# Chunk-selected attention into a gated causal convolution: from merged step lists to a list-scheduled graph, with the convolution in sixteen 32x32 array tiles

## The chip, the core and the metric

The kernel runs on one core of a Trainium2 chip. TensorE (PE) multiplies matrices, with weight loads of its own (PEld); VectorE (DVE), ScalarE (ACT) and GpSimd (POOL) work elementwise; SyncE (SP) issues the DMAs. PE writes to PSUM, eight banks of 512 fp32 numbers on each of 128 partitions, from which DVE and ACT read. The metric is the time of one execution on the device in microseconds.

## The reference

Inputs are q, k, v of shape (4, 8, 768, 64) and the weights w_val, w_out (512x512) and conv_w (5x512). Keys are cut into 24 chunks of 32. Each query takes the six chunks with the highest upper bound among its causal ones, and attends to their keys:

```python
k_min, k_max = k_chunks.min(3), k_chunks.max(3)
ub = sum(maximum(q * k_min, q * k_max), axis=-1)       # per query and chunk
ub = where(causal, ub, -1e9);  top_chunks = argsort(ub)[..., -6:]
scores = q @ k.T / 8;  mask = (chunk of key in top_chunks) & causal
x = softmax(where(mask, scores, -1e9)) @ v             # heads side by side: (4, 768, 512)
gate = sigmoid(sum_k conv_w[k] * x shifted by 4 - k)   # per channel, causal
out = (gate * (x @ w_val)) @ w_out
```

## The kernel before

The 32 heads are worked off as 16 pairs, two heads of one batch side by side on 128 partitions (64 each). Four pairs make a batch, whose 512 channels are four blocks of 128.

For each pair, `kq_steps` transposes k and q on PE in fp32 (lines 155 and 178). ACT copies keys, scaled, into KE (159) and q into q32 (181), GpSimd casts q to fp16 into QU (183) and v into VA (190), and DVE reduces each chunk of keys to maximum and minimum straight from PSUM (163, 164) and makes of them the fp32 operand KB (170, 172). `sel_steps` computes all bounds with fp32 matmuls (207 with relu(q), 209 with q), takes the eight highest with `max` (219), compares with the sixth (224), transposes the 0/1 result (233) and copies it into the free rows of QU (236). There it meets the rows of KE that hold -30 for each chunk, so that the score matmul (271) adds the penalty of chunks that are not selected. `attn_steps` takes exp of a 512-column bank at a time (275, 295), GpSimd zeroes the triangle above the diagonal (264, 280), `av` multiplies with v and a column of ones (304), DVE divides (306, 307), and six transposes put the pair into xT (314, 316).

For each batch, `moe_gate` does the convolution on PE: five taps, each a diagonal 128x128 matrix in two fp16 parts (high and rest), so ten accumulating matmuls of 384 columns for each block and half of the sequence (334); ACT takes tanh (339). `moe_val` multiplies with w_val (348) and DVE forms the gate product (352). `moe_out` multiplies with w_out (359), ACT evacuates (362), SP stores (363). The 40 diagonals are built once by GpSimd in `moe_diag` (379), ten in each of the first four pairs; the cast of the weights is also GpSimd's (366, 367).

The order of the work is written by hand: `merge` interleaves the step lists of the attention of pair i, the selection of pair i+1, the transposes of pair i+2 and the batch steps due then, by their relative place in each list. PSUM has three pools: three banks for scores, two for AV, three for all the rest. Six loads for each pair are issued by SP, two pairs ahead.

Of the kernel before, what the change touches and what calls it, by code (L numbers as in the profile page):

```python
# [13 lines left out]
AX = mybir.AxisListType  # L14


@with_exitstack
def kernel(
# [10 lines left out]
    nc = tc.nc  # L29
# [8 lines left out]
    PEN = -30.0  # L38
    NPAIR = (B * H) // 2
    HB = S // 2  # L40


    HP = (slice(0, 64), slice(64, 128))
    CP = (slice(64, 64 + NCH), slice(0, NCH))
    KP = (slice(0, 64 + NCH), slice(0, 128))

    CC = (1, 0)
    SELT = NT - 1

    ident_np = np.eye(128, dtype=np.float32)  # L50
    identh_np = np.eye(128, dtype=np.float16)
    e_np = np.zeros((64, S), dtype=np.float16)
    for c in range(NCH):
        e_np[c, c * CH:(c + 1) * CH] = PEN
    cfill_np = np.zeros((128, SELT, 2, NCH), dtype=np.float32)
    for it in range(1, NT):
        for p in range(128):
            cfill_np[p, it - 1, :, (it * 128 + p) // CH + 1:] = -1.0e9
    cfill_np = cfill_np.reshape(128, SELT * 2 * NCH)

    ident_dr = nc.inline_tensor(ident_np, name="identc")
    identh_dr = nc.inline_tensor(identh_np, name="identh")
    e_dr = nc.inline_tensor(e_np, name="echunk")
    cfill_dr = nc.inline_tensor(cfill_np, name="cfill")

    cpool = ctx.enter_context(tc.tile_pool(name="cpool", bufs=1))
    npool = ctx.enter_context(tc.tile_pool(name="npool", bufs=3))
    hpool = ctx.enter_context(tc.tile_pool(name="hpool", bufs=2))
    ppool = ctx.enter_context(tc.tile_pool(name="ppool", bufs=2))
    mpool = ctx.enter_context(tc.tile_pool(name="mpool", bufs=2))  # L70
    ps = ctx.enter_context(tc.tile_pool(name="ps", bufs=3, space=bass.MemoryType.PSUM))

    ident = cpool.tile([128, 128], FP, tag="ident")
    identh = cpool.tile([128, 128], F16, tag="identh")
    cfill = cpool.tile([128, SELT * 2 * NCH], FP, tag="cfill")
    wval_sb = cpool.tile([128, NCT, DM], F16, tag="wval")
    wout_sb = cpool.tile([128, NCT, DM], F16, tag="wout")
    w32 = cpool.tile([128, 2, NCT, DM], FP, tag="w32")
    cwn = cpool.tile([KSZ * NCT, 128], FP, tag="cwn")
    cwT = cpool.tile([128, KSZ * NCT], FP, tag="cwT")  # L80
    cwh = cpool.tile([128, KSZ * NCT], F16, tag="cwh")
    cwl = cpool.tile([128, KSZ * NCT], FP, tag="cwl")
    diag = cpool.tile([128, KSZ * NCT, 2, 128], F16, tag="diag")
    xT = cpool.tile([128, 2 * NCT, S + 4], F16, tag="xT")
    KE = [cpool.tile([128, 2, S], F16, tag=f"KE{i}", name=f"KE{i}") for i in range(3)]
    QU = [cpool.tile([128, 2, S], F16, tag=f"QU{i}", name=f"QU{i}") for i in range(3)]
    VA = [cpool.tile([128, 2, NT, D + 1], F16, tag=f"VA{i}", name=f"VA{i}") for i in range(3)]
    KB = [cpool.tile([128, 2, 2 * NCH], FP, tag=f"KB{i}", name=f"KB{i}") for i in range(2)]
    NS = [cpool.tile([128, SELT, 128], F16, tag=f"NS{i}", name=f"NS{i}") for i in range(2)]

    def bank(shape, dt=FP, tag="w", bufs=3):
        return ps.tile(shape, dt, tag=tag, name=f"ps_{tag}", bufs=bufs)

    nat = {}

    def load_kq(p):
        b, h0 = p // NCT, 2 * (p % NCT)
        kn = npool.tile([128, NT, 128], FP, tag="kn", name="kn")
        qn = npool.tile([128, NT, 128], FP, tag="qn", name="qn")
        vn = npool.tile([128, NT, 128], FP, tag="vn", name="vn")  # L100
        nat[p] = (kn, qn, vn)
        for t, src in ((kn, k), (qn, q)):
            for hh in range(2):
                nc.sync.dma_start(out=t[:, :, hh * 64:(hh + 1) * 64],
                                  in_=src[b, h0 + hh].rearrange("(t p) d -> p t d", p=128))

    def load_v(p):
        b, h0 = p // NCT, 2 * (p % NCT)
        for hh in range(2):
            nc.sync.dma_start(out=nat[p][2][:, :, hh * 64:(hh + 1) * 64],  # L110
                              in_=v[b, h0 + hh].rearrange("(t p) d -> p t d", p=128))


    nc.sync.dma_start(out=ident, in_=ident_dr.ap())
    load_kq(0)
    for i in range(3):
        for hh in range(2):
            nc.sync.dma_start(out=KE[i][HP[1 - hh], hh, :], in_=e_dr.ap())
    nc.sync.dma_start(out=cfill, in_=cfill_dr.ap())
    nc.sync.dma_start(out=identh, in_=identh_dr.ap())  # L120
    load_v(0)
    load_kq(1)
    load_v(1)
    nc.sync.dma_start(out=cwn, in_=moe_conv_w.rearrange("k (c p) -> (k c) p", p=128))
    nc.sync.dma_start(out=w32[:, 0], in_=moe_w_val.rearrange("(ct c) e -> c ct e", c=128))
    nc.sync.dma_start(out=w32[:, 1], in_=moe_w_out.rearrange("(et e) o -> e et o", e=128))

    for i in range(2):
        nc.gpsimd.memset(KB[i], 0.0)
    for i in range(3):  # L130
        nc.vector.memset(QU[i][HP[1], 0, :], 0.0)
        nc.vector.memset(QU[i][HP[0], 1, :], 0.0)
    for i in range(2):
        nc.gpsimd.memset(NS[i], 0.0)
    for i in range(3):
        nc.gpsimd.memset(VA[i][:, :, :, D:D + 1], 1.0)
    nc.vector.memset(xT[:, :, 0:4], 0.0)

    st = {}


    def kq_steps(p):
        kn, qn, vn = nat.pop(p)
        ke, qu, va, kb = KE[p % 3], QU[p % 3], VA[p % 3], KB[p % 2]
        kmx = hpool.tile([128, NCH], FP, tag="kmx", name="kmx")
        kmn = hpool.tile([128, NCH], FP, tag="kmn", name="kmn")
        kmd = hpool.tile([128, NCH], FP, tag="kmd", name="kmd")
        q32 = hpool.tile([128, S], FP, tag="q32", name="q32")
        rq = hpool.tile([128, S], FP, tag="rq", name="rq")
        st[p] = dict(ke=ke, qu=qu, va=va, kb=kb, q32=q32, rq=rq)  # L150

        def khalf(w):
            pt = bank([128, HB])
            for tl in range(3):
                nc.tensor.transpose(out=pt[:, tl * 128:(tl + 1) * 128],  # L155
                                    in_=kn[:, 3 * w + tl, :], identity=ident)
            sl = slice(w * HB, (w + 1) * HB)
            for hh in range(2):
                nc.scalar.activation(out=ke[HP[hh], hh, sl], in_=pt[HP[hh]],  # L159
                                     func=AF.Copy, scale=0.125)  # L160
            cs = slice(w * 12, (w + 1) * 12)
            ptc = pt.rearrange("p (c t) -> p c t", t=CH)
            nc.vector.tensor_reduce(out=kmx[:, cs], in_=ptc, axis=AX.X, op=ALU.max)  # L163
            nc.vector.tensor_reduce(out=kmn[:, cs], in_=ptc, axis=AX.X, op=ALU.min)

        def kblock():
            nc.vector.tensor_tensor(out=kmd, in0=kmx, in1=kmn, op=ALU.subtract)
            for hh in range(2):
                hp, c0 = HP[hh], CC[hh] * NCH
                nc.vector.tensor_scalar(out=kb[hp, 0, c0:c0 + NCH], in0=kmd[hp],  # L170
                                        scalar1=kmd[hp, 0:1], scalar2=None, op0=ALU.subtract)
                nc.vector.tensor_scalar(out=kb[hp, 1, c0:c0 + NCH], in0=kmn[hp],
                                        scalar1=kmn[hp, 0:1], scalar2=None, op0=ALU.subtract)

        def qhalf(w):
            pt = bank([128, HB])
            for tl in range(3):
                nc.tensor.transpose(out=pt[:, tl * 128:(tl + 1) * 128],  # L178
                                    in_=qn[:, 3 * w + tl, :], identity=ident)
            sl = slice(w * HB, (w + 1) * HB)  # L180
            nc.scalar.activation(out=q32[:, sl], in_=pt, func=AF.Copy)  # L181
            for hh in range(2):
                nc.gpsimd.tensor_copy(out=qu[HP[hh], hh, sl], in_=q32[HP[hh], sl])  # L183
            a = max(w * HB, 128)
            nc.vector.tensor_scalar(out=rq[:, a:(w + 1) * HB], in0=q32[:, a:(w + 1) * HB],
                                    scalar1=0.0, scalar2=None, op0=ALU.max)

        def vcast():
            for hh in range(2):
                nc.gpsimd.tensor_copy(out=va[:, hh, :, 0:D],  # L190
                                      in_=vn[:, :, hh * 64:(hh + 1) * 64])

        return [lambda: khalf(0), lambda: khalf(1), lambda: qhalf(0), kblock, lambda: qhalf(1),
                vcast]
# [254 lines left out]
```

## Time and profile before

| | |
|---|---|
| median of 3 runs | 294.87 us (294.83 to 296.1) |
| profiled execution, first to last instruction | 292.5 us |
| median less that span | 2.4 us |
| mean granted TensorE clock | 0.959 |
| PE busy / PEld busy | 241.3 / 171.6 us |
| DVE / ACT / POOL busy | 155.2 / 160.2 / 121.8 us |
| read and written in HBM | 21.79 and 6.29 MB |

The profiled execution has its span as its own time; the runs' times include what lies around it. Lines such as L334 are lines of the kernel before. A group's row gives the operation, its output and input, its count, then its busy time in us, the mean ns of one, and the idle time in front with what ended it. Matmuls are pipelined: the mean of one is its latency, and the price of one in a row of many is read from a timeline, as length over count.

### The profile page before, as it was taken

The numbers are of one execution on the slowest core, as the hardware profiler recorded it, in microseconds if no ns is written. First come the engines' busy times: TensorE is split into PE (matmuls) and PEld (weight loads), VectorE is DVE, ScalarE is ACT, GpSimd is POOL, SyncE is SP. The second block draws the span as 40 slices with busy tenths as digits, with TensorE's granted clock in tenths as the row PEclk, the third lists the DMA queues.
The fourth block names the chain that finished last, engine by engine and source line by source line (L and its number), as shares of the span: only waits on it lengthen the run. The fifth ranks groups of instructions, "written<-read, shape, count | busy, mean of one in ns | idle before, by whom it ended". The sixth has DMA issues, their size and how long they took to land.

```text
span 292.5 us, 5928 instructions
## 1 busy us (share of the span) xinstructions
PE 241.3 (82%) x2161; PEld 171.6 (59%) x2161; DVE 155.2 (53%) x522; ACT 160.2 (55%) x329; POOL 121.8 (42%) x261
## 2 busy tenths in 40 slices
PE   2383926509998897999998999999989999999994
PEld 1181614405757575776666667676757676765551
DVE  3547162404676674858573657666645667631160
ACT  3232713503768659465674774756747765467313
POOL 2416189999254436243433253425251624223000
PEclk9999975956999999999999999999999999999999
DMA  7999992205162554242456343332211000003105
GB/s 165 211 304 245 218 175 54 54 0 110 33 132 55 110 110 99 66 108 56 107 151 159 91 114 86 70 87 61 74 74 38 36 2 0 2 2 143 73 2 215
DMA packets 80746, 28.46 MB, mean 97 GB/s; under 512 B 75962, under 2 KB 76622, under 8 KB 80718
## 3 DMA queue, kind: packets, MB, share of 16 engines
q1 hardware_dynamic: 80718, 28.09, 40.9%
q8 instruction: 17, 0.28, 0.4%
q14 instruction: 11, 0.09, 0.1%
HBM read 21.79 MB, written 6.29 MB: 96 GB/s over the span
## 4 chain that ended last, share of the span: by engine, by line
PE 66%; POOL 12%; ACT 10%; issue 3%; SPq 3%; DVE 2%; DMA 2%; ACTq 0%; POOLq 0%
PE ps_w L334 17%; PE ps_s L271 10%; POOL diag L379 7%; PE ps_av L304 6%; PE ps_w L348 6%; PE ps_w L359 6%; PE ps_w L209 6%; ACT P L275 5%; PE ps_w L207 5%; PE ps_w L155 4%; PE ps_w L178 2%; POOL QU L183 2%; PE ps_w L314 2%; ACT KE L159 2%; ACT osb L362 1%
## 5 line engine op out<-in xcount | busy, mean ns | idle before, releaser
L275 ACT ACTIVATE P<-ps_s 128x512 f16<-128x512 f32 x160 | 87.8, 606 | 57.1 <-PE ps_s L271 56.8
L271 PE MATMUL ps_s<-QU,KE 88*128 88x512 f16 (+5 forms) x224 | 54.9, 336 | 7.1 <-ACT P L275 4.1
L264 POOL TENSOR_SCALAR_AFFINE_SELECT P<-P 128x256 f16<-128x256 f16 (+1 forms) x80 | 29.0, 364 | 71.1 <-ACT P L275 58.3
L334 PE MATMUL ps_w<-xT,diag 128*128 128x384 f16 x320 | 57.8, 331 | 0.0
L304 PE MATMUL ps_av<-VA,P 128*128 128x65 f16 x672 | 33.4, 196 | 21.9 <-POOL P L264 19.9
L304 PEld LDWEIGHTS <-P 128*128 128x128 f16 x672 | 28.4, 99 | 32.0 <-POOL P L264 26.2
L159 ACT ACTIVATE KE<-ps_w 64x384 f16<-64x384 f32 x64 | 31.0, 485 | 26.9 <-PE ps_w L155 26.5
L183 POOL CAST QU<-q 64x384 f16<-64x384 f32 x64 | 35.1, 548 | 24.6 <-ACT q L181 22.7
L334 PEld LDWEIGHTS <-diag 128*128 128x128 f16 x320 | 31.0, 99 | 21.4 <-issue 1.9
L339 ACT ACTIVATE g<-ps_w 128x384 f32<-128x384 f32 x32 | 15.9, 498 | 30.5 <-PE ps_w L334 30.5
L209 PE MATMUL ps_w<-KB,q 128*128 128x48 f32 x160 | 32.3, 285 | 0.0
L163 DVE TENSOR_REDUCE kmx<-ps_w 128x12 f32<-128x384 f32 x32 | 17.8, 555 | 26.7 <-ACT KE L159 26.6
L236 DVE COPY QU<-ps_w 24x640 f16<-24x640 f16 x32 | 15.5, 484 | 29.9 <-PE ps_w L233 29.4
L207 PE MATMUL ps_w<-KB,rq 128*128 128x48 f32 x160 | 31.2, 278 | 0.0
L271 PEld LDWEIGHTS <-KE 88*128 88x128 f16 (+1 forms) x224 | 21.1, 101 | 16.8 <-issue 10.8
L280 POOL TENSOR_SCALAR_AFFINE_SELECT P<-P 128x256 f16<-128x256 f16 x32 | 13.1, 408 | 31.4 <-ACT P L275 31.3
L207 PEld LDWEIGHTS ps_w<-KB,rq 128*128 128x128 f32 x160 | 25.9, 202 | 0.3
L155 PE MATMUL ps_w<-ident,kn 128*128 128x128 f32 x96 | 17.7, 300 | 9.7 <-DMA kn<-in_k_dram 9.7
L209 PEld LDWEIGHTS ps_w<-KB,q 128*128 128x128 f32 x160 | 25.7, 202 | 0.0
L348 PE MATMUL ps_w<-xT,wval_sb 128*128 128x384 f16 x128 | 23.9, 325 | 1.8 <-ACT q L181 1.8
L190 POOL CAST VA<-vn 128x384 f16<-128x384 f32 x32 | 16.5, 516 | 20.4 <-PE ps_av L304 12.9
L359 PE MATMUL ps_w<-wout_sb,gv 128*128 128x512 f16 x96 | 23.8, 379 | 0.7 <-ACT osb L362 0.7
(46 smaller groups left out, 309.0 us busy)
## 6 DMA issues: line engine op xcount, KB each, us to landing
kn<-in_k_dram SPq DMA_DIRECT2D x32, 192.0 KB, 3.3
qn<-in_q_dram SPq DMA_DIRECT2D x32, 192.0 KB, 3.4
vn<-in_v_dram SPq DMA_DIRECT2D x32, 192.0 KB, 3.3
out_dram<-osb SPq DMA_DIRECT2D x24, 256.0 KB, 2.0
w<-in_moe_w_val_dram SPq DMA_DIRECT2D x1, 1024.0 KB, 5.6
w<-in_moe_w_out_dram SPq DMA_DIRECT2D x1, 1024.0 KB, 7.9
KE<-echunk SPq DMA_DIRECT2D x6, 96.0 KB, 2.7
cfill<-cfill SPq DMA_DIRECT2D x1, 120.0 KB, 2.3
```

The source lines that it names most:

```text
L155: nc.tensor.transpose(out=pt[:, tl * 128:(tl + 1) * 128], in_=kn[:, 3 * w + tl, :], identity=ident)
L159: nc.scalar.activation(out=ke[HP[hh], hh, sl], in_=pt[HP[hh]], func=AF.Copy, scale=0.125)
L183: nc.gpsimd.tensor_copy(out=qu[HP[hh], hh, sl], in_=q32[HP[hh], sl])
L207: nc.tensor.matmul(out=pu[:, it - 1, :], lhsT=rq[:, ts], rhs=kb[:, 0, :], start=True, stop=False)
L209: nc.tensor.matmul(out=pu[:, it - 1, :], lhsT=q32[:, ts], rhs=kb[:, 1, :], start=False, stop=True)
L264: nc.gpsimd.affine_select(out=ap, in_=ap, pattern=[[0, n], [1, 128]], compare_op=ALU.is_ge, fill=0.0, base=0, channel_multiplier=-1)
L271: nc.tensor.matmul(out=pq[:, col:col + n], lhsT=ke[KP[hh], hh, jt * 128:(jt + 1) * 128], rhs=qu[KP[hh], hh, q0:q0 + n], start=True, stop=True)
L275: nc.scalar.activation(out=pt, in_=pq, func=AF.Exp)
L304: nc.tensor.matmul(out=pav[:, qt, :], lhsT=where[hh, jt, qt], rhs=va[:, hh, jt, :], start=(jt == 0), stop=(jt == qt))
L334: nc.tensor.matmul(out=pg, lhsT=diag[:, ki * NCT + ct, part, :], rhs=xT[:, slot, w * HB + ki:w * HB + ki + HB], start=(n == 0), stop=(n == ...
L348: nc.tensor.matmul(out=pv, lhsT=wval_sb[:, ct, et * 128:(et + 1) * 128], rhs=xT[:, slot0 + ct, 4 + w * HB:4 + (w + 1) * HB], start=(ct == ...
L359: nc.tensor.matmul(out=po, lhsT=gv[b, et][:, s * 128:(s + 1) * 128], rhs=wout_sb[:, et, :], start=(et == 0), stop=(et == NCT - 1))
```

## The change

The kernel is written anew. Every operation is added to a `Plan` as a node with an engine, a duration and a latency (constants in the file), a priority (pair number times `PERIOD` plus an offset for its kind from `OFF`), the tiles that it reads and writes, and the PSUM banks that it takes. `Plan.schedule` places the nodes one after another: of those ready on an engine, the earliest, by priority among equals; banks are given out of all eight as nodes need them. The instructions are then emitted in the order of their planned starts.

```diff
+    def schedule(self):
...
+                if best is None or t < best[0]:
+                    best = (t, n, pick)
...
+        return sorted(done, key=lambda n: (n.start, n.i))
...
+    order = plan.schedule()
+    with tc.manual_schedule():
+        for n in order:
+            n.fn()
-    merge(kq_steps(0))
-    merge(sel_steps(0), kq_steps(1))
```

The convolution waits for all four pairs of a batch, takes four banks, and runs as 160 matmuls for each half of the sequence, each on a 32x32 tile of the array. Row tile r takes channels 32r to 32r+31 of each block; column tile c is block c; each row tile writes its own bank. So gate channels come out in another order, and the columns of w_val and the rows of w_out are permuted to match when they are cast and loaded. The diagonals shrink to 32x32 and are built by DVE in two instructions.

```diff
-                    nc.tensor.matmul(out=pg, lhsT=diag[:, ki * NCT + ct, part, :],
-                                     rhs=xT[:, slot, w * HB + ki:w * HB + ki + HB],
-                                     start=(n == 0), stop=(n == 2 * KSZ - 1))
+                for n in range(2 * KSZ):
+                    ki, part = n // 2, n % 2
+                    for r in range(4):
+                        rp = slice(32 * r, 32 * r + 32)
+                        for c in range(4):
+                            nc.tensor.matmul(out=psum[32 * c:32 * c + 32, gb[r // 2].at + r % 2, 0:HB],
+                                             lhsT=diag[rp, part, ki * NCT + c, :],
+                                             rhs=xT[rp, s0 + c, hw * HB + ki:hw * HB + ki + HB],
+                                             start=(n == 0), stop=(n == 2 * KSZ - 1))
```

The bounds are computed in fp16: q is split into a high part QH and a rest QL, relu(q) into RH and RL, the key bounds likewise, and six matmuls of 48 columns for each of five query tiles (two for the first) replace two fp32 ones.

```diff
-                nc.tensor.matmul(out=pu[:, it - 1, :], lhsT=rq[:, ts], rhs=kb[:, 0, :],
-                                 start=True, stop=False)
-                nc.tensor.matmul(out=pu[:, it - 1, :], lhsT=q32[:, ts], rhs=kb[:, 1, :],
-                                 start=False, stop=True)
+                for lhs, part, kind in ((QH, 0, 1), (RH, 0, 0), (QH, 1, 1), (RH, 1, 0), (QL, 0, 1), (RL, 0, 0)):
+                    term(it, lhs, kbs(part, kind), n == 0, n == 5)
```

Who does what also moves. ACT evacuates keys and q in one 768-column instruction each; DVE reduces keys from that SBUF copy; GpSimd scales it into KE; DVE makes QH, RH, RL and QU, GpSimd QL:

```diff
+            add(f"ke{h}_{p}", POOL, t_pool(S), 100, base + OFF["KE"] + h,
+                lambda h=h: nc.gpsimd.tensor_scalar(out=KE[t3][HP[h], h, :], in0=K32[w][HP[h]],
+                                                    scalar1=0.125, scalar2=None, op0=ALU.mult),
...
+            lambda: nc.vector.tensor_copy(out=QH[w], in_=Q32[w]), [("Q32", w)], [("QH", w)])
...
+            lambda: nc.gpsimd.tensor_tensor(out=QL[w][:, 128:S], in0=Q32[w][:, 128:S],
+                                            in1=QH[w][:, 128:S], op=ALU.subtract),
```

Maxima and comparison read the bounds in PSUM, and the future chunks are filled there by one small addition. The two heads' score banks lie side by side, so exp takes 1024 columns at once (six instructions for a pair, eleven before), one GpSimd instruction zeroes the triangles of both heads, and one DVE instruction each divides, and forms the gate product for both halves. A 33rd selection row carries a shift of the scores by the row's highest bound; the first query tile, which had no selection, has it now too. One of the two mask copies is ACT's. Identities, chunk rows and fill are made on GpSimd, not loaded. Eight matmuls on zeros stand in front. Input tiles have four buffers, loads are issued up to 3.85 periods ahead, the weights' loads at 4.94 periods.

## The prediction

> **What bounds the kernel now.** I read the busy times first, then the table of windows, which says in which stage an engine is full, then the timeline of one steady stretch for the price of each operation. The page:
>
> ```profile
> PE 241.3 (82%) x2161; PEld 171.6 (59%) x2161; DVE 155.2 (53%) x522; ACT 160.2 (55%) x329; POOL 121.8 (42%) x261
> ```
>
> The 82% is a mean over unlike stages. The windows (length, then busy time of each engine) separate them:
>
> ```profile
> core 0: us, PE busy (x) PEld busy (x) DVE busy (x) ACT busy (x) POOL busy (x), PEclk, DMA share, GB/s
> 0.00:27.10 27.10, 10.99 (x50) 9.25 (x51) 14.51 (x43) 7.02 (x13) 10.04 (x24) 1.00 1.03 232
> 27.10:65.50 38.40, 19.18 (x150) 13.83 (x150) 11.56 (x46) 14.42 (x30) 29.56 (x54) 0.76 0.61 107
> 123.80:183.70 59.90, 56.73 (x542) 41.15 (x540) 37.95 (x129) 39.26 (x84) 23.28 (x53) 1.00 0.43 107
> 183.70:243.70 60.00, 56.82 (x543) 41.14 (x541) 37.25 (x130) 39.36 (x84) 23.00 (x52) 1.00 0.19 54
> 274.80:292.50 17.70, 13.67 (x77) 7.23 (x74) 4.44 (x8) 5.16 (x9) 0.00 (x0) 1.00 0.32 120
> ```
>
> Three stages: a start, in which PE is half idle up to 65.5 us (chain first, then GpSimd, 29.56 of 38.40 us); a steady part of 60 us for each batch of four pairs, in which PE is 95% busy and the others at two thirds or less; a tail. In the steady part removed PE work is removed time. Its prices, from the chain and the timeline (start, length, what):
>
> ```profile
> 123.81 3.26 PE ps_w L334 x20
> 127.34 0.66 PE ps_av L304 x21
> 132.26 1.31 PE ps_w L348 x8
> 204.92 0.86 PE ps_w L359 x4
> ```
>
> ```profile
> 129.60 0.50 PE L155 MATMUL ps_w<-ident,kn 128*128 128x128 f32 x3
> 129.93 0.32 PE L207 MATMUL ps_w<-KB,rq 128*128 128x48 f32 x2
> 132.10 1.47 PE L348 MATMUL ps_w<-xT,wval_sb 128*128 128x384 f16 x8
> ```
>
> So a 384-column matmul takes 163 ns, a 512-column one 216, an AV matmul (65 columns, with its own weight load) 31.5, an fp32 transpose 110 (129.60 to 129.93), and the bound matmuls of a pair 2.17 us (129.93 to 132.10). Last, two rows for the engines that share memory with each other:
>
> ```profile
> L379 POOL TENSOR_SCALAR diag<-identh,cwT 128x128 f16<-128x128 f16 x20 | 12.9, 647 | 0.0
> L185 DVE TENSOR_SCALAR rq<-q x32: 273/375/2045, 9.1 to 244.9; 128x256 f32<-128x256 f32 x16, 128x384 f32<-128x384 f32 x16
> ```
>
> The forty diagonal builds are what starves PE in the second window. The 2045 ns of a copy whose median is 375 falls beside GpSimd's 2067 ns cast of the weights: VectorE's plain SBUF copies stand still while GpSimd holds that memory.
>
> **Part by part.** *PE for a pair, before:* 12 fp32 transposes 1.32, bounds 2.17, five selection transposes 0.28, scores 2.28 (twice 2,688 columns at 0.42 ns), AV 42 x 31.5 = 1.32, six transposes 0.34: 7.7 us. A batch adds the convolution 80 x 163 = 13.0, value 32 x 163 = 5.2 and output 24 x 216 = 5.2, so 4 x 7.7 + 23.4 = 54.2 us of the 59.9: PE works 0.91 of the steady stretch by these prices.
>
> *Bounds in fp16 halves:* 32 fp16 matmuls of 48 columns with 128-column weights replace ten fp32 ones. Nearest row is AV: 32 x 31.5 = 1.0 us, 1.2 less. With six selection transposes, a pair costs 6.6 us; 16 pairs 105.8.
>
> *The convolution:* 40 full matmuls for each half of a sequence and channel block become 160 matmuls for all four blocks, each 32x32 with its own 32-column weight load; 1280 in all. No row shows such a tile. If all 16 stream together, ten rounds of 163 ns make 10.2 ns each; if they are limited by issuing load and matmul, the nearest row is AV's 31.5, an upper bound in so far as its load is four times wider; if they run one after another, 163. I take 26, by AV's row less something for the narrower load: 1280 x 26 = 33.3 us against 52.2 now. Ends 13 and 40 if they overlap; 209 if not.
>
> The order of emission walks the four column tiles inside a row group. In the trace of before all 128x128 weight loads overlap matmuls on the same rows: the 20 convolution matmuls above take 163 ns each with a 99 ns load in front of every one. The Trainium skill, "TensorE: Matmul & The Clock Gate", section "The mechanism", says that a load overlaps matmuls in flight only when its row group differs (or goes into the background weights), which speaks against this order: read strictly, the four columns of a row group would run in turn. By the rule alone, as an estimate with this trace's 163 ns, a tile would cost at least 41 ns if row groups still overlap, 52 us in all and 19 more than my term. Its section "Measured speedup vs the span model" has 16 tiles at 10.6 times the speed of single ones, which no row here shows.
>
> *Value and output* keep 20.9 and 20.7 us. PE in all: 105.8 + 33.3 + 41.6 = 180.7 us against 217 before.
>
> *ACT for a pair:* two 768-column evacuations, six exps (five of 1024, one of 256), a mask copy, a share of tanh and output. From 128x512 exps in a row, 2.07 us for four, 0.49 each, and 0.86 ns per further column (606 less 386 ns for 512 and 256), that is 0.70 x 3 + 4.9 + 1.4 = 8.4 us. Fewer, larger instructions; off the path.
>
> *DVE for a pair:* two 768-element reductions from SBUF (0.47 per 384 by their step) 1.9, key bounds five small ones 0.8, three fp16 casts of q's halves and one threshold copy 1.7 to 2.6, the low part 0.8, fill and maxima 1.1, compare 0.4, mask 0.56, AV scaling 1.15, xT 0.56, gate product 0.95: 9 to 10 us. That is under the steady PE need of a pair (45.2 / 4 = 11.3) but over the 6.6 of the first five pairs, in front of which no convolution stands.
>
> *POOL for a pair:* two key scalings 64x768 (two casts of 384 at 0.55, less one overhead: 0.95) 1.9, low part 640 elements 1.0 to 1.6, value cast 0.95, four triangles 2.1, one small: 6.2 to 6.8 us. The triangles keep their place between exp and AV. The diagonals move to DVE, two instructions of 640 elements, and the 26 us of GpSimd before 65.5 us vanish. What is late next there is DVE.
>
> *DMA:* input issues stay six a pair on SP, with four buffers; e-chunk, masks and identities are no longer loaded but made on GpSimd (some 8 us: four 64x768 selects at 1.0, memsets), beside the first loads. The weights' loads are moved on SP behind the keys of the ninth pair, whose buffer comes free when the fifth pair's keys are transposed; the first convolution, right after the fifth pair's AV on PE, waits for them, and behind it everything on PE: that has a load (5.6 us from issue to landing before) and diagonals to fit into one pair's time, and costs nothing if it does, some 5 us if not (in the range). Output stores stand between loads on SP, as before.
>
> *Start:* keys land at 5 us as now (first PE record 5.22); transposes cold 1.3, evacuation 0.9, reductions 1.9, key bounds 0.8; meanwhile GpSimd's key scaling 1.9 and low part 1.5, DVE's 0.8, then bounds 1.6 cold, fill to compare 1.8, transposes 0.5, mask 0.7: first scores near 18 us, now at 27.07.
>
> *Sum.* 18 us hold 4.6 us of PE work (five sets of six transposes, one pair's bounds and selection). The tail after the last pair is a convolution 8.3, value 5.2, output 5.2 = 18.7, with 1.5 for tanh and gate between, and 2.7 for the last evacuation and store. The middle: 180.7 - 4.6 - 18.7 = 157.4 at the 0.91 of before, 173. Together 18 + 173 + 18.7 + 1.5 + 2.7 = 213.9 us of span. Before, the span is 292.5 us and the median 294.87, so 2.4 lie around it: **216 us**.
>
> **Rivals.** *VectorE and GpSimd bound it.* Four of DVE's copies for a pair are of the kind that waited above, and GpSimd now works over half of the time; at 0.4 us each DVE needs 10 + 1.6 = 11.6 a pair. If the key scaling runs nearer to L379's tensor-scalar row (647 ns for 128 elements) than to a cast, GpSimd passes 12. Then 18 + 16 x 11.8 + 22.9 + 2.4 = 232, and up to 250 when PE waits on them in the chain as well. For it: the 2045 ns. Against it: steady DVE is at 63%.
>
> *The tiles do not overlap: slower.* If each 32x32 matmul streams its 384 columns alone, the convolution costs 209 us, 175 over my term: 391 us, with PE full and all else idle in stretches of 26 us for each half. It decides from 26 + (294.9 - 216) / 1280 x 1000 = 88 ns for a tile. This is also the case that the change doesn't do what it says. Against it: loads and matmuls overlap well in the full array; for it: no row has a tile.
>
> *Better than that.* Tiles at 15 ns (14 us less) and a middle at 0.95 (7 less): 195.
>
> **How the numbers follow.** Forecast case 0.62 (200 to 232), VectorE and GpSimd 0.20 (232 to 252), better 0.08, tiles that don't overlap 0.10. The range from 200 to 252 holds the first two. Faster by over 0.5% (about what a measurement can tell here) is all but the last, 0.89; same 0.01; slower 0.10.
>
> **What would show it.** Right: two groups of 160 convolution matmuls for a batch, each about 4 us; first score near 18 us; no GpSimd stretch that starves PE; PE over 85% of the span's middle; 32 bound matmuls in 1.0 us. Wrong: convolution groups of over 10 us; gaps on PE that end with DVE's QH, QU or RL copies, or with GpSimd's KE and QL; a granted clock that falls in the tiled stretches.

## The result and the profile after

The changed kernel takes 255.93 us (median of 4 runs, 253.21 to 256.82) against 294.86 before: ratio 0.866, 95% interval 0.861 to 0.872. It is faster, as forecast, but 40 us over the forecast 216 and 4 us above the range. Times here are medians of all runs of a kernel; ratios and their intervals leave out runs over 1.5% longer than the fastest of the same kernel (two of four in e4, one each in e2, e6 and e7). The profiled execution has a span of 254.8 us. Busy times:

```profile
PE 194.1 (76%) x3337; PEld 139.4 (55%) x3337; DVE 196.5 (77%) x505; ACT 149.0 (58%) x182; POOL 156.5 (61%) x174
```

PE lost 47 us of work, as meant; VectorE and GpSimd gained 41 and 35. The windows, cut at the first scores, at the start and end of the first convolution, at the start of the second one's last part and at the start of the tail; of the late middle two rows are shown, from the end of the second convolution to the third, and the last stretch in front of the tail:

```profile
core 0: us, PE busy (x) PEld busy (x) DVE busy (x) ACT busy (x) POOL busy (x), PEclk, DMA share, GB/s
0.00:26.50 26.50, 12.87 (x76) 8.31 (x77) 20.93 (x48) 5.33 (x7) 20.17 (x31) 0.69 1.23 204
26.50:90.10 63.60, 47.69 (x630) 36.94 (x630) 58.60 (x168) 45.04 (x52) 52.06 (x50) 0.88 0.89 173
90.10:98.60 8.50, 5.60 (x328) 4.18 (x328) 8.35 (x16) 2.12 (x3) 6.93 (x12) 0.90 0.02 6
98.60:154.80 56.20, 47.06 (x724) 35.43 (x721) 50.36 (x142) 40.26 (x50) 42.37 (x43) 0.91 0.46 104
163.70:203.30 39.60, 32.97 (x494) 24.21 (x492) 34.15 (x92) 30.34 (x38) 26.76 (x30) 1.00 0.10 35
215.40:231.20 15.80, 15.80 (x221) 10.46 (x230) 7.37 (x12) 12.00 (x16) 3.24 (x7) 1.00 0.19 68
231.20:254.80 23.60, 16.45 (x384) 9.53 (x381) 5.89 (x7) 6.61 (x10) 0.00 (x0) 1.00 0.31 113
```

Where PE was 95% busy before, it now is at 75 and 84% up to 154.8 us, and VectorE is at 92% and 90%. Behind the second convolution they are nearly even (83% and 86%), and only the last 15.8 us in front of the tail have PE full. PE is also granted less clock in the first two of these stretches (0.88 and 0.91; 0.906 over the span, 0.959 before). The chain that ended last (shares by engine), and the group that GpSimd adds to it:

```profile
PE 38%; DVE 27%; POOL 19%; issue 8%; ACT 3%; DMA 3%; SPq 1%; POOLq 0%; ACTq 0%; DVEq 0%
...
L438 POOL TENSOR_SCALAR KE<-K 64x768 f16<-64x768 f32 x32 | 69.4, 2169 | 22.1 <-PE psum L575 20.6 <-ACT K L414 0.2
```

One stretch on the timelines of GpSimd and PE shows how GpSimd holds PE up:

```profile
51.23 4.70 POOL L438 TENSOR_SCALAR KE<-K 64x768 f16<-64x768 f32 x2
56.00 1.96 POOL L596 TENSOR_SCALAR_AFFINE_SELECT P<-P 128x256 f16<-128x256 f16 x4
56.47 1.25 PE L605 MATMUL psum<-VA,P 128*128 128x65 f16 x34 [3.89 <-POOL P L596]
```

Two key scalings (L438) stand in GpSimd's queue in front of the triangles (L596), and PE stands still for 3.89 us until the first triangle is done. The chain's 3% of DMA are the weights' load; its end falls beside this wait by the profile's times, but the first instruction that reads these weights, a cast, starts at 89.2 us, so nothing stood waiting for them here.

Last, the first convolution on the chain, and the instruction queues of the DMA:

```profile
90.14 2.74 PE psum L652 x135
92.88 0.61 issue
93.49 1.72 PE psum L652 x128
95.21 2.28 issue
97.49 0.70 PE psum L652 x34
```

```profile
q8 instruction: 26, 0.43, 0.7%
```

The tiles do stream together: 128 of them in 1.72 us, 13.4 ns each, where one 384-column matmul of the full array takes 163. Between the groups PE stands still, for 0.6 and 2.3 us here. A group of 128 is 256 instructions, a weight load and a matmul each. The records of that DMA queue are 16,384 bytes apiece, and three of them start at 91.11, 95.09 and 98.60 us, beside these pauses. Their number follows PE's instructions: 26 records for 2 x 3337 loads and matmuls, which is 26 times 256, and 17 before for 2 x 2161.

### The profile page after: what moved, and what is told of

It reads as the page before. It is cut to its first block, busy times and chain, and to the rows that moved or that the text cites. A ratio compares the mean times of both kernels' runs of the same rounds, so it can differ in the third digit from the quotient of the medians.

```text
span 254.8 us, 8024 instructions
## 1 busy us (share of the span) xinstructions
PE 194.1 (76%) x3337; PEld 139.4 (55%) x3337; DVE 196.5 (77%) x505; ACT 149.0 (58%) x182; POOL 156.5 (61%) x174
## 4 chain that ended last, share of the span: by engine, by line
PE 38%; DVE 27%; POOL 19%; issue 8%; ACT 3%; DMA 3%; SPq 1%; POOLq 0%; ACTq 0%; DVEq 0%
POOL KE L438 10%; PE psum L672 7%; PE psum L652 6%; PE psum L693 5%; PE psum L575 5%; DVE KK L419 5%; PE psum L409 4%; POOL P L596 4%; PE psum L605 4%; DVE KB L429 3%; DVE TOP L510 3%; DMA w<-in_moe_w_val_dram 3%; PE psum L533 3%; DVE QU L454 2%; DVE KB L432 2%
## 5 line engine op out<-in xcount | busy, mean ns | idle before, releaser
L582 ACT ACTIVATE P<-psum,bias 128x1024 f16<-128x1024 f32 x96 | 90.2, 1011 | 10.9 <-PE psum L575 10.3
L438 POOL TENSOR_SCALAR KE<-K 64x768 f16<-64x768 f32 x32 | 69.4, 2169 | 22.1 <-PE psum L575 20.6
L575 PE MATMUL psum<-QU,KE 97*128 97x512 f16 (+7 forms) x256 | 50.4, 317 | 3.5 <-ACT P L582 2.1
L596 POOL TENSOR_SCALAR_AFFINE_SELECT P<-P 128x512 f16<-128x512 f16 (+1 forms) x64 | 34.2, 553 | 30.3 <-ACT P L582 29.4
L605 PE MATMUL psum<-VA,P 128*128 128x65 f16 x672 | 28.6, 200 | 14.3 <-POOL P L596 10.9
L605 PEld LDWEIGHTS <-P 128*128 128x128 f16 x672 | 26.5, 102 | 19.4 <-POOL P L596 12.0
L575 PEld LDWEIGHTS <-KE 97*128 97x128 f16 (+1 forms) x256 | 22.7, 101 | 15.1 <-issue 6.8
L457 POOL TENSOR_TENSOR QL<-Q,QH 128x640 f16<-128x640 f32 x16 | 23.7, 1479 | 10.0 <-DVE QH L448 5.0
L419 DVE TENSOR_REDUCE KK<-K 128x24 f32<-128x768 f32 x32 | 29.4, 942 | 0.3 <-ACT K L414 0.2
L652 PE MATMUL psum<-xT,diag 32*32 32x384 f16 x1280 | 18.5, 338 | 11.7 <-issue 10.5
L672 PE MATMUL psum<-xT,wval 128*128 128x384 f16 x128 | 25.6, 354 | 1.3 <-issue 1.3
L414 ACT ACTIVATE K<-psum 128x768 f32<-128x768 f32 x16 | 12.9, 808 | 23.3 <-PE psum L409 22.6
L661 ACT ACTIVATE G<-psum 128x768 f32<-128x768 f32 x16 | 12.2, 808 | 21.8 <-PE psum L652 21.8
L693 PE MATMUL psum<-wout,GV 128*128 128x512 f16 x96 | 23.5, 378 | 0.0
L444 ACT ACTIVATE Q<-psum 128x768 f32<-128x768 f32 x16 | 12.9, 805 | 14.1 <-PE psum L409 14.1
```

What stands on the lines that cost most here:

```text
L419: lambda i=i, op=op: nc.vector.tensor_reduce(out=KK[w][:, i, :], in_=K32[w].rearrange("p (c t) -> p c t", t=CH), axis=AX.X, op=op), [("K32 ...
L438: lambda h=h: nc.gpsimd.tensor_scalar(out=KE[t3][HP[h], h, :], in0=K32[w][HP[h]], scalar1=0.125, scalar2=None, op0=ALU.mult),
L457: lambda: nc.gpsimd.tensor_tensor(out=QL[w][:, 128:S], in0=Q32[w][:, 128:S], in1=QH[w][:, 128:S], op=ALU.subtract),
L575: nc.tensor.matmul(out=psum[:, bk.at + h, col:col + m], lhsT=KE[t3][KP[h], h, jt * 128:jt * 128 + 128], rhs=QU[t3][KP[h], h, q0:q0 + m], s ...
L582: add(f"e{nm}_{p}", ACT, t_act(2 * n), 124, pr, lambda pt=pt, bk=bk, n=n: nc.scalar.activation(out=pt[:, :, 0:n], in_=psum[:, bk.at:bk.at ...
L596: nc.gpsimd.affine_select(out=ap, in_=ap, pattern=pat, compare_op=ALU.is_ge, fill=0.0, base=0, channel_multiplier=-1)
```

## Experiments

The theory after the result: the sum of PE's work was right, but VectorE and GpSimd set the time of the middle; GpSimd by its key scaling, VectorE by standing behind GpSimd's instructions. The main rival: PE with its pauses and its lower clock. Times are medians; "before" stands at 292.9 to 296.5 us in all these runs.

| run | time, us | ratio to before, 95% interval |
|---|---|---|
| e1_key_cast | 240.18 | 0.816 (0.810 to 0.821) |
| e2_key_on_act | 258.45 | 0.877 (0.871 to 0.883) |
| e3_full_conv | 279.15 | 0.947 (0.941 to 0.954) |
| e4_tiles_by_column | 253.40 | 0.854 (0.846 to 0.861) |
| e5_no_key_work | 237.84 | 0.807 (0.803 to 0.811) |
| e6_copies_on_act | 245.97 | 0.833 (0.827 to 0.838) |
| e7_rows_late | 242.04 | 0.819 (0.813 to 0.824) |
| e8_true_key_price | 261.85 | 0.890 (0.884 to 0.896) |
| e9_no_key_min | 237.46 | 0.807 (0.801 to 0.812) |
| e10_two_rounds | 227.30 | 0.772 (0.768 to 0.776) |
| e11_no_low_part | 232.94 | 0.790 (0.785 to 0.796) |
| e12_relief | 227.21 | 0.771 (0.766 to 0.776) |
| e13_half_columns | 276.40 | 0.941 (0.935 to 0.946) |
| e14_bounds_on_act | 239.60 | 0.814 (0.809 to 0.819) |

### GpSimd's key scaling

```diff
-                lambda h=h: nc.gpsimd.tensor_scalar(out=KE[t3][HP[h], h, :], in0=K32[w][HP[h]],
-                                                    scalar1=0.125, scalar2=None, op0=ALU.mult),
+                lambda h=h: nc.gpsimd.tensor_copy(out=KE[t3][HP[h], h, :], in_=K32[w][HP[h]]),
...
-                out=pt[:, :, 0:n], in_=psum[:, bk.at:bk.at + 2, 0:n], func=AF.Exp, bias=bias),
+                out=pt[:, :, 0:n], in_=psum[:, bk.at:bk.at + 2, 0:n], func=AF.Exp, bias=bias, scale=0.125),
```

> GpSimd makes KE by a plain cast; the factor 1/8 moves into the scale of exp, and the chunk rows of KE are eight times larger; the result is the same and the order of emission unchanged. Theory (GpSimd's key scaling at 2.17 us instead of 0.95, and VectorE standing behind GpSimd, took what PE gave): KE drops to about 0.9 us each, GpSimd's busy time from 156 to about 115 us, VectorE's by 10 to 20 us, and the time from 256 to 225 to 238 us. Rival (PE is the bound of the middle, by the tiles' stalls and a lower granted clock): within 2% of 256 us.

The same data moved by a cast instead of a multiplication; the group, and the chain of this run:

```profile
L438 POOL CAST KE<-K 64x768 f16<-64x768 f32 x32 | 27.9, 870 | 21.8 <-PE psum L574 20.7 <-ACT K L414 0.2
```

```profile
DVE 49%; PE 31%; issue 9%; ACT 7%; POOL 3%; DVEq 0%; ACTq 0%; POOLq 0%
```

870 ns instead of 2169, and 15.75 us less time. GpSimd leaves the chain (19% to 3%) and VectorE takes half of it. The theory holds, with less than it asked for: VectorE's busy time fell by 6.7 us, not 10 to 20. This version beats both kernels and does the same computation; it is the base of most runs below.

```diff
-        add(f"ke{h}_{p}", POOL, t_pool(S), ...  nc.gpsimd.tensor_scalar(
+        add(f"ke{h}_{p}", ACT, t_act(S), ...  nc.scalar.activation(
```

> KE is scaled by ScalarE from the SBUF copy, planned as such; GpSimd does no key work. Theory: GpSimd's busy time falls to about 88 us, VectorE's small copies QU, KB, RH fall towards their shortest durations (total VectorE 196 to about 170 us), ScalarE's rises from 149 to about 175, time 222 to 236 us. Rival (only GpSimd's own length counted, VectorE is not slowed by it): VectorE's busy time stays within 5 us of 196. Rival (PE bound): time within 2% of 256.

GpSimd fell to 88.0 us and VectorE to 180.5, so VectorE is slowed by GpSimd's work; but nothing was won. The plan ordered everything anew, ScalarE's busy time rose to 175.4, and its exps lead the list of the chain's lines (11%). A miss of the theory's time, and not clean: engine and order changed together.

> The changed kernel's instructions unaltered, with GpSimd's slow key scaling; only the plan is told its measured price, 2100 ns instead of 879, and so orders anew. Theory (the time is set by the work of VectorE and GpSimd): 256 changes by less than 6 us. Rival (it was the order, made for a wrong price, that cost): 10 us or more are won.

```diff
-            add(f"ke{h}_{p}", POOL, t_pool(S), ...
+            add(f"ke{h}_{p}", POOL, 2100.0, ...
```

261.85 us: 5.9 more by the medians, 7 by the ratios, so at the edge of what the theory allowed or past it, and not the gain that the rival asked for. The wrong price in the plan did not cost the time by its order. But the run also shows that another order of the same instructions is worth 6 us, which bears on every run with a new plan, e2 above all.

> As the key cast on GpSimd (240.2 us), but from the fourth pair on the cast is left out altogether: KE keeps the keys of the first three pairs. GpSimd loses 26 casts of 0.87 us. Theory (VectorE bounds the middle, by its own work and by standing behind GpSimd): the part that stood behind these casts goes, about 5 us of VectorE's busy time, and the time falls by 3 to 8 us, to 232 to 237. Rival (GpSimd's own queue bounds it): it falls by over 12 us, to 228 or less.

With 26 casts gone (22.6 us of GpSimd) only 2.3 us are won, which is not what the rival asked for and also less than the theory did (3 to 8), though VectorE's busy time fell by 5.5 as expected: once it is a cast, GpSimd's own queue is not the limit.

### VectorE

> As the key cast on GpSimd (240.2 us), but the second key reduction (the minimum, 0.94 us of VectorE, 0.89 from start to start) is left out from the third pair on: 14 reductions. Nothing else moves to another engine. Theory (VectorE bounds the stretches in front of the convolutions): 7 to 13 us less, 227 to 233. Rival (VectorE is busy but does not bound, PE or the order does): 2 us less or nothing.

2.7 us for 14 reductions: the rival's side, nearly, and a miss of the theory. VectorE's busy time fell by 6.9 us only, though 14 reductions are 13.2: other instructions took longer in their place (the difference of the key bounds, KK, from 4.1 to 6.4 us, QH from 8.9 to 10.0). VectorE led the chain of e1 (49%), but here PE is close behind it (40% to 44%).

> As the key cast on GpSimd, but GpSimd's subtraction for the low part of q (QL, 1.48 us) is left out from the third pair on: 14 of them; everything that reads QL stays. VectorE's own work is unchanged. Theory (VectorE's time behind GpSimd is what can be won back): the 12 us that its instructions end with a QL go from its busy time, and 6 to 12 us from the time, 228 to 234. Rival (the waiting is hidden): within 3 us of 240.

7.2 us, as the theory said, without a change to VectorE's own work; its busy time falls from 189.8 to 178.4. Two other readings weigh little: RL, which reads QL, had 0.1 us of idle time in front of it in all of e1, and taking 22.6 us of other work out of GpSimd's queue (e5) won 2.3.

> As the key cast on GpSimd, with the two small casts of key bounds (KB, 64x48, 0.16 us at their shortest but 0.46 on average on VectorE) issued by ScalarE, which shares nothing with GpSimd. If VectorE's standing behind GpSimd belongs to these instructions, its busy time falls by 12 to 15 us and the time by 4 to 8, to 232 to 236. If the next instruction of VectorE waits in their place, its busy time falls by 5 to 8 us and the time by 0 to 3.

```profile
L432 DVE TENSOR_TENSOR KB<-KK,KB 64x48 f16<-64x48 f32 x32 | 15.9, 498 | 7.8 <-ACT KB L429 7.0
```

VectorE 8.2 us less, time 0.6 us less: the second reading. In e1 this subtraction took 333 ns on average; now it is the one that waits behind GpSimd.

> As the key cast on GpSimd, and the xT copies and VectorE's mask copies (32 of 0.56 us, 18 us of VectorE) are issued by ScalarE at the same places of the same plan. Theory (VectorE bounds the middle): 240.2 falls by 6 to 14 us, to 226 to 234. Rival (PE bounds it): within 2 us of 240, or slower, since a copy takes 0.80 us on ScalarE.

5.8 us slower, though VectorE lost 13.9 us: the theory missed, and "slower" is what the rival allowed. ScalarE gained 23.1, and its share of the chain went from 7% to 24%, its exps and these copies in front (12%, 6% and 3%). So the run does not say whether VectorE is a limit; it shows that another engine's queue is no free place.

> Three omissions together, on the key cast (240.2 us): no key minimum, no QL from the third pair on, no key cast from the fourth on. Alone they won 2.7, 7.2 and 2.3 us. If the engines in front of PE share the limit, and PE is next at once, together they win about their sum, 10 to 14 us: 226 to 230. If each was capped by the other two, they win more than the sum: the PE sum of the prediction with the late start, 216 + 8 = 224, or less. If something else (start, tail, the convolutions' lumps) sets the rest: no more than e11 alone, 232 to 234.

13.0 us, where the three alone gave 12.2: their sum, not more, so none of the three had been hidden behind the others. PE's work is the same as in e1, and PE now leads the chain:

```profile
PE 48%; DVE 23%; ACT 13%; issue 11%; POOL 3%; ACTq 0%; DVEq 0%; POOLq 0%
```

### The start

> As the key cast on GpSimd, but VectorE's six copies of the chunk rows into KE stand in front of the mask copy of the pair that needs them, not in front of the first key reduction. Theory (the first scores were late because the reductions stood behind these copies, and these behind GpSimd's chunk rows): first scores at 20 to 22 us instead of 25.5, time 3 to 6 us less, 234 to 237. Rival (what VectorE saves at the start it lacks later): first scores earlier, time within 2 us of 240.

First scores at 23.91 us instead of 25.53, later than the 20 to 22 of the theory, and no time won: the rival. The timeline of VectorE at the start of the changed kernel, with GpSimd's beside it, shows what made it late:

```profile
7.55 4.36 DVE L303 COPY KE<-etile 64x768 f16<-64x768 f16 x6 [3.09 <-POOL etile L297]
8.49 4.51 POOL L438 TENSOR_SCALAR KE<-K 64x768 f16<-64x768 f32 x2
...
11.83 1.79 DVE L419 TENSOR_REDUCE KK<-K 128x24 f32<-128x768 f32 x2
...
14.25 1.49 POOL L457 TENSOR_TENSOR QL<-Q,QH 128x640 f16<-128x640 f32 x1 [1.25 <-DVE KK L422]
14.40 2.15 DVE L429 CAST KB<-KK 64x48 f16<-64x48 f32 x2
```

The first reduction, whose keys had been in place since 7.2 us, stands behind six copies of chunk rows, these behind GpSimd's making of them; then two casts of 48 columns take 2.15 us beside QL. With the copies moved, KB casts and subtractions at 10.59 and 12.76 take 2.14 and 1.64 us, and two of the copies take 2.35 us at 20.91, right in front of the mask copy that the first scores need: the wait moved with the queue.

### The convolution's tiles

> The convolution goes back to 128x128 diagonals (forty 384-column matmuls for each half of a sequence and all blocks: 40 x 163 = 6.5 us a half, where the tiles took 6.2 to 8 us for both halves together), same order of nodes, diagonals of 2560 columns built by VectorE. If PE is not the bound of the middle, the 22 us more of PE work cost 5 to 12 us: 261 to 268 us. If PE is the bound: 276 to 282 us. If the tiles are no gain with their stalls: 256 or less.

23.2 us more than the changed kernel: the second case, as if PE were the bound. One convolution is 80 matmuls in a lump of 13 us; the first one takes 15.85, with a granted clock of 0.50 up to 97.9 us:

```profile
92.47 15.85 PE L644 MATMUL psum<-xT,diag 128*128 128x384 f16 x80
```

The four convolutions take 55.5 us here and 30.2 in the changed kernel, so the lumps count nearly in full, although VectorE is the busier engine between them. (VectorE's two builds of the larger diagonals also take 5.6 us instead of 1.6.)

> As the key cast on GpSimd, with two of the ten accumulating rounds of the convolution: 256 tile matmuls instead of 1280, VectorE's and ScalarE's work as before. The four convolutions take about 7.5 us each with their stalls now; with 64 matmuls each they would take 1 to 1.5. If each lump counts in full: 22 to 26 us less, 214 to 218. If VectorE's work covers the lumps of the middle and only the last one, in the tail, counts: 6 to 10 us less, 230 to 234.

12.9 us, halfway between the two expectations: of some 24 us of lumps about half counts in the faster base. The rest is probably taken up by waits for other engines: inside the first convolution PE now stands 3.2 us for VectorE's division (ON).

> The two inner loops of the convolution are exchanged: four row tiles of one column tile follow each other, instead of four column tiles of one row tile. If loads of the same row group wait for matmuls in flight, the bursts of 128 matmuls (1.72 us now) get shorter and the time falls by 2 us or more; if not, the bursts stay at 13 to 14 ns for a matmul, the stalls of 2.3 us between them stay, and the time is the same within its interval.

```profile
93.42 1.71 PE L652 MATMUL psum<-xT,diag 32*32 32x384 f16 x128 [1.56 <-issue]
```

The burst of 128 takes 1.71 us, as in the other order (1.72), and the pauses stay. The time is 2.5 us less by the medians (ratio 0.854 against 0.866), but the two intervals touch at 0.861; whether the order of loops matters at all is not settled, only that it does not change the burst.

> As the key cast on GpSimd, but nine of the ten rounds of the convolution go in matmuls of 192 columns instead of 384: 304 load-and-matmul pairs instead of 160 for each half, with the same columns streamed. If the stalls of 2 us after every 128 pairs come from loading code (256 instructions), a convolution of 7.5 to 8.5 us becomes 15 to 18 us, with a stall after every 128 pairs, and the time grows by 15 to 35 us, to 255 to 275. If they come from the tiles or the streamed columns, it stays at 7.5 to 10 us and the time at 240 to 248.

```diff
-                            nc.tensor.matmul(out=psum[32 * c:32 * c + 32, gb[r // 2].at + r % 2, 0:HB],
+                            for q0, m in ((0, HB),) if n == 0 else ((0, HB // 2), (HB // 2, HB // 2)):
+                                nc.tensor.matmul(out=psum[32 * c:32 * c + 32, gb[r // 2].at + r % 2, q0:q0 + m],
```

```profile
150.59 2.11 PE L652 MATMUL psum<-xT,diag 32*32 32x192 f16 x128 [1.31 <-issue]
154.31 2.46 PE L652 MATMUL psum<-xT,diag 32*32 32x192 f16 x128 [1.62 <-issue]
157.77 2.28 PE L652 MATMUL psum<-xT,diag 32*32 32x192 f16 x128 [1.00 <-issue]
```

The same columns in nearly twice the instructions: 36 us more, of which the four convolutions make 35 (65.0 us against 30.3 in e1), a group of 128 every 3.5 to 3.7 us though each has half the columns, and the 16 KB records of the instruction queue at the same steps (148.0, 151.7, 155.5, 158.8 us). There are 35 records now, for 2 x 4489 loads and matmuls, again one for 256. The clock is no rival: it was 0.50 from 151.0 to 164.6 us, which makes the bursts longer, but the step is that of the changed kernel, where the pauses stand at full clock too. The pauses are code loading.

## Why the prediction was wrong, by its steps

**The convolution term was right in size, by luck.** 26 ns a tile and 33.3 us were predicted; the first convolution takes 8.05 us for 320 tiles (90.14 to 98.19), 25 ns each, and the four together 30.2. The reason given for the value, an issue limit near AV's, was not the mechanism: bursts at 13.4 ns and pauses for code. The slower rival, tiles in turn, fell: e3 puts the gain of the tiles at 23 us. The Trainium skill's rule that a load overlaps matmuls in flight only when its row group differs ("TensorE: Matmul & The Clock Gate", "The mechanism"), read strictly, shows nowhere in the bursts, in neither order of loops; the same section lets a load go ahead into the background weights, and no run here tells whether that is the reason. The Trainium skill, "Runtime: NRT & Kernel Launch", section "Instruction fetch mechanics", has code refilled in blocks of 256 instructions, as seen here, and the fetch hidden behind the issue of instructions; here it is not, since 256 instructions are gone in 1.72 us and a block comes every 3.4 to 4.0. Two readings of the text are off without moving its sum: the forty full matmuls are those of half a sequence for all four blocks, not for each, and the diagonals took 24.9 us of GpSimd, not 26.

**The bounds were right:** 32 matmuls in 0.82 us warm (1.0 predicted). **The tail was right:** 23.6 us against 22.9. **The weights' loads** cost nothing, one of the two cases that the prediction allowed.

**The start was mis-sized by 8.5 us:** 26.5 against 18. The step put GpSimd's chunk rows "beside the first loads" and forgot that VectorE copies them into KE, in front of the first reduction, and that key scaling and QL stand in VectorE's way there. Placing 8.5 us here is bookkeeping: e7 started the scores 1.6 us earlier and won nothing.

**The middle is the step that failed.** From the first scores to the tail it took 231.2 - 26.5 = 204.7 us against 173: 31.7 over, so that with 8.5 and 0.7 the whole miss of 40.9 us of span is placed. The sum divided PE's work by the 0.91 of before, a share that belongs to a stretch in which PE led. The text itself had VectorE at 9 to 10 us a pair (its terms add up to 9.9 to 10.8) against 6.6 of PE in the first five pairs, and did not carry it into the sum: those five took 63.6 us, with 11.7 of VectorE's busy time a pair, where PE's work at 0.91 would be 36. A stage's time is at least that of its busiest engine, and each stage has its own.

That the other engines' work is what filled the middle is shown by runs that leave PE's work alone. From the first scores to the last convolution it takes 204.6 us in the changed kernel (26.53 to 231.10), 188.6 in e1 with the cheap cast (25.53 to 214.13) and 175.5 in e12, which also leaves out work of VectorE and GpSimd (25.53 to 201.01). The last is nearly the 173 of the sum: with the two engines relieved, PE did its work at about the share that the sum had supposed. The lumps of the convolution on PE and its clock still have a part in the time (e3, e10).

**Two prices under it were too low.** GpSimd's scaling was priced as a cast, 0.95 us, though the nearest operation in the trace, L379's tensor-scalar with 647 ns for 128 elements, said otherwise and was left to a rival; it takes 2.17, never under 2.12, and e1 puts 15.75 us on it. VectorE's instructions were priced by their own length. Adding up, for all of VectorE's instructions, what each takes over the shortest of its form gives 44 us in the changed kernel, 38 in e1, 22 in e12 and 17 before. Most of that (some 31 us in the changed kernel and in e1) ends together with a GpSimd instruction, QL above all in e1; e11 wins 7.2 us by leaving QL out.

The Trainium skill, "SBUF — State Buffer", section "Who interferes with whom", has a mechanism for this: VectorE's copies and casts in a two-port mode contend with GpSimd for shared ports, operations with two SBUF inputs do so with GpSimd's reads, whoever issues first holds the ports for a whole instruction, and reductions never contend. The trace agrees: the key casts of 48 columns go from 0.16 to 1.41 us here; the key reduction, 0.94 on average, never takes more than 0.96.

**The rival that came true** was the one of VectorE and GpSimd (0.20, up to 252): its mechanism was right (it had VectorE at 11.6 us a pair, and the first five took 11.7), its price 4 us short; the late start and the lumps of the convolution on PE were not in its sum. Its bound is no single engine: e9 and e5 each relieve one and win little, e12 wins the sum of three, and PE comes next at once. How much of the remaining 227 us is the order's lack of slack, and how much PE's lower clock, was not separated.

## What to carry to other kernels

When an edit takes work from the bound engine and gives it to the others, make the sum anew for each stage with every engine in it, and take the largest; the old engine's share of busy time does not survive the edit. Price a moved operation by the nearest row of the same operation on that engine, not of the same data. A stream of many small matmuls should be looked at in instructions: here the loading of code set the pace at 26 to 31 ns for a load and a matmul, and the instruction queue's DMA records say so.

## What the runs showed of the hardware

- Code for PE came in blocks of 16 KB, 256 instructions, 3.4 to 4.0 us apart when PE was waiting for it: 26 to 31 ns for a load-and-matmul pair, no more than an AV pair takes (31.5 ns). A burst on code already there ran at 13.4 ns a pair.
- GpSimd's multiplication by a constant took 2.5 times its cast of the same tile (2169 and 870 ns), and VectorE is not the reason: the shortest of 32 took 2121 and 816.
- An instruction of VectorE of 0.16 us can take 1.4 us beside GpSimd; taken away, the next one takes the wait (333 to 498 ns in e14).
- PE's granted clock fell to 0.50 for 13.6 us or more from within each convolution of e13, whose pauses are the most (0.862 over the span). The tiles alone do not explain a low clock: 0.906 with them, 0.908 in e3 without, 0.971 in e14 with them, 0.959 before.
